# Loading and converting the f64 weights of a fused attention, FFN and MoE kernel in pairs of pieces

## The chip, the cores and the metric

The kernel runs on one core of a Trainium2 chip. The metric is the device time of one execution in microseconds (us). Engine names: PE is TensorE, DVE is VectorE, ACT is ScalarE, POOL is GpSimd, SP is SyncE, which issues nearly all DMAs here.

## The reference

Three stages follow one another. `moe_w_in` and `moe_w_out` arrive as f64, all else as f32.

```python
# attention: q, k, v are (4, 8, 576, 64); a mask lets block i of 64 rows see blocks 0..i
scores = scale * np.matmul(q, k.transpose(0, 1, 3, 2))
attn = exp(scores - max) / (sum + 1e-09);  x = attn @ v        # -> 2304 tokens x 512
# dense FFN: w_in (512, 2048), w_out (2048, 512), both f64
h = x @ w_in;  g = where(h > 0, h, exp(min(h, 0)) - 1);  x = g @ w_out
# MoE: tokens with x @ w_skip > 0 go to the best of 8 experts, the others pass through
out[do_compute] = xc + gate_w * (relu(xc @ w1[e]) @ w2[e])
```

## The kernel before

**Stages.** Tokens go through the FFN in nine chunks of 256 (`c` = 0 to 8). Attention is cut into units of one batch, head pair and block pair, which run between the matmuls of the FFN chunks. The experts follow, in a tail of their own. Chunk 0 and chunk 1 use the f32 weights directly (`twi`, `two` as lhs or rhs of f32 matmuls, PE groups `h<-xt,twi` and `y<-two,g`). From chunk 2 on, the weights are split into f16 high and low parts (`win`, `wout`), and a matmul becomes three f16 ones.

**The raw weights.** An f64 is two int32 words. Each of the 16 weight blocks `j` (eight of `w_in`, eight of `w_out`) is loaded raw in two pieces of 512 KB, so there are 32 pieces `x`. `raw_load` (L460) issues one on SP into a place of 128 x 1024 int32: three places that serve any piece (two buffers of the tag `pay`, one of `wt`), and eight (`wo0` to `wo7`) that are later the targets of the `w_out` blocks and may serve pieces before that. A piece of `w_in` has all 512 rows and 128 columns, so its contiguous runs are 1 KB; one of `w_out` has 128 whole rows, runs of 4 KB. `conv` (L486) makes 512 f32 columns of a piece with three DVE instructions, one `TENSOR_SCALAR` and two `SCALAR_TENSOR_TENSOR`. Each of the last two reads what the one before it wrote. Within a block, the first half of the columns is ready when its own piece is converted.

**What sets the order.** The program is not run in the order in which it is written. Every operation is recorded with an estimated duration (`Recorder`, L35), and `Recorder.order` (L152) lists them anew per engine from the dependences, the estimates and a due time that follows the place in the program. Each engine then runs its own list strictly in order, and waits at the head of it block all behind. `conv_step` (L1291) records a conversion and the loads around it: it runs at most five pieces ahead. A load of piece `x` that is recorded after the conversion of piece `x-4` waits for that conversion (end of `raw_load`).

**Around it.** SP's list mixes the raw weight pieces with `raw<-in_q/k/v` (f32 rows of 64, runs of 256 bytes), the DMA transposes `kt`, `qt`, `et` and `x2t`, the copies `qt<-qt`, and `vflat`, a whole batch of `v` that ACT squares and sums (`vmax`, L621) so that `vscale(1)` (L631) can take a maximum on DVE (`col<-col`). `l2` (L923) multiplies block `f` of `g` by block `f` of `w_out` for both halves of the tokens. `post` (L943) writes the chunk's rows through a `pay` buffer. `ahead_gather` (L1080) uses one `pay` buffer between the posts of chunk 7 and of chunk 8.

```python
def conv_step():                       # L1291
    x = nload[0]
    load_to(x + 1)
    conv(x)
    load_to(min(nraw[0] + 2, x + 5))
    nload[0] += 1
```

Of the kernel before, what the change touches and what calls it, by code (L numbers as in the profile page):

```python
# [347 lines left out]
def tile_kernel(ctx, tc, q, k, v, w_in, w_out, w_skip, w_gate, w1, w2, out):  # L348
# [109 lines left out]
    CONV = {}  # L458

    def raw_load(x):  # L460

        if not RING:
            RING.append(True)
            RFREE.extend((99, pool.tile([128, 1024], I32, tag=tag, bufs=bufs, name="rw")) for pool, tag, bufs in ((mo, "pay", 2), (mo, "pay", 2), (wp, "wt", 1)))
            RFREE.extend((16 + 2 * i, wp.tile([128, 1024], I32, tag=f"wo{i}", bufs=1, name="rw")) for i in range(8))
        ok = [r for r in RFREE if r[0] > x]
        if not ok:
            return False
        place = min(ok, key=lambda r: r[0])
# [16 lines left out]
    def conv(x):  # L486

        j, m = divmod(x % 16, 2)
        kind = "wi" if x < 16 else "wo"
        if m == 0:  # L490
            TW[kind, j] = wp.tile([128, 1024], I32, tag=f"{kind}{j}", bufs=1, name=f"t{kind}{j}")
        t = TW[kind, j]
        place = RAWW.pop(x)
        RFREE.append(place)
        raw = place[1].rearrange("p (f two) -> p f two", two=2)
        lo, hi = raw[:, :, 0], raw[:, :, 1]
        if kind == "wi":
            dst = t.rearrange("p (k f) -> p k f", k=4)[:, :, m * 128:(m + 1) * 128]
            lo, hi = (a.rearrange("p (k f) -> p k f", k=4) for a in (lo, hi))
        else:  # L500
            dst = t[:, m * 512:(m + 1) * 512]
        rc.vector.tensor_scalar(out=dst, in0=hi, scalar1=0x07FFFFFF, scalar2=3, op0=ALU.bitwise_and, op1=ALU.logical_shift_left)
        rc.vector.scalar_tensor_tensor(out=dst, in0=hi, scalar=-(1 << 30), in1=dst, op0=ALU.bitwise_and, op1=ALU.bitwise_or)
        rc.vector.scalar_tensor_tensor(out=dst, in0=lo, scalar=29, in1=dst, op0=ALU.logical_shift_right, op1=ALU.bitwise_or)
        CONV[x] = len(rc.steps) - 1

# [35 lines left out]
    def split_win(j):  # L542
        t = wp.tile([128, 2, 1024], F16, tag="wt" if j == 0 else f"wi{j - 1}", bufs=1, name=f"win{j}")
# [32 lines left out]
    def split_wout(j):  # L576
        t = wp.tile([128, 2, 1024], F16, tag="wi7" if j == 0 else f"wo{j - 1}", bufs=1, name=f"wout{j}")
# [209 lines left out]
    def h_unit(b, p, i):  # L787
# [14 lines left out]
        elif HL.get(("wo", 7)) is not None and nu[0] % 3 == 0:  # L802
            pool, tag, bufs = wp, "wo7", 1
        else:
            pool, tag, bufs = ap, "ehl", 2
        HP[b, p, x] = pool.tile([128, n, nk, 2, 128], F16, tag=tag, bufs=bufs, name="ehl")
# [537 lines left out]
    for x in range(8):  # L1344
# [607 lines left out]
```

## Time and profile before

| | |
|---|---|
| runs shown | 752.17, 742.56, 750.12 us; median 750.12 us |
| the profiled execution | 746.02 us, of which the span of the trace is 743.9 us |
| mean granted TensorE clock | 0.968 of full speed |
| PE busy | 679.4 us (91% of the span) |
| DVE, ACT busy | 578.7 us (78%), 513.9 us (69%) |
| DMA | 134.52 MB, mean 181 GB/s |

The span falls into three stretches. Up to some 140 us the weights are loaded and chunk 0 runs. From there to some 580 us PE is busy nearly without a break. The experts' tail fills the rest. A busy engine is not yet the one that sets the time: for that, the rows below say what each wait ended with.

### The profile page before, as it was taken

The numbers are of one execution on the slowest core, as the hardware profiler recorded it, in microseconds if no ns is written. First come the engines' busy times: TensorE is split into PE (matmuls) and PEld (weight loads), VectorE is DVE, ScalarE is ACT, GpSimd is POOL, SyncE is SP. The second block draws the span as 40 slices with busy tenths as digits, with TensorE's granted clock in tenths as the row PEclk, the third lists the DMA queues.
The fourth block names the chain that finished last, engine by engine and source line by source line (L and its number), as shares of the span: only waits on it lengthen the run. The fifth ranks groups of instructions, "written<-read, shape, count | busy, mean of one in ns | idle before, by whom it ended". The sixth has DMA issues, their size and how long they took to land.

```text
span 743.9 us, 17734 instructions
## 1 busy us (share of the span) xinstructions
PE 679.4 (91%) x6665; PEld 466.1 (63%) x6665; DVE 578.7 (78%) x1664; ACT 513.9 (69%) x1090; POOL 83.4 (11%) x122
## 2 busy tenths in 40 slices
PE   4689997999999899999999999989999989997894
PEld 3467543775476657657657658657575768675673
DVE  5987989897899797989869966999687634554752
ACT  5876656999797785788758846775365727685782
POOL 2000000010000100000100010100113124143211
PEclk9669999899999999999999999999999999999998
DMA  9999999967787989699656559726267486799941
GB/s 271 270 262 294 292 280 207 203 119 149 145 170 147 172 177 198 122 172 195 112 90 135 90 96 281 277 78 207 57 199 211 124 180 138 200 244 252 272 127 16
DMA packets 267355, 134.52 MB, mean 181 GB/s; under 512 B 234539, under 2 KB 243765, under 8 KB 266736
## 3 DMA queue, kind: packets, MB, share of 16 engines
q1 hardware_dynamic: 263056, 125.69, 72.7%
q0 software_dynamic: 4192, 7.49, 4.7%
q8 instruction: 57, 0.93, 0.5%
q14 instruction: 50, 0.41, 0.2%
HBM read 74.38 MB, written 12.75 MB: 117 GB/s over the span
## 4 chain that ended last, share of the span: by engine, by line
PE 45%; DMA 19%; issue 16%; DVE 12%; ACT 3%; POOL 2%; SPq 1%; POOLq 0%; another core or an unknown queue 0%; DVEq 0%; ACTq 0%
PE h L310 18%; PE y L310 17%; DMA et<-ehl 6%; DMA gp<-pay_d,lists 5%; PE s L310 4%; PE xps L310 3%; DVE ehl L310 2%; DMA rw<-in_moe_w_out_dram 2%; DMA out_dram<-o,gp 2%; DVE two L310 1%; DVE mx L310 1%; DMA vflat<-in_v_dram 1%; POOL out_dram L1684 1%; DMA lst_d<-li,si 1%; DVE el L310 1%
## 5 line engine op out<-in xcount | busy, mean ns | idle before, releaser
L310 PE MATMUL h<-xt,win 128*128 128x256 f16 x1344 | 158.7, 273 | 2.2 <-DVE el L310 2.1
L310 PE MATMUL y<-wout,g 128*128 128x512 f16 x672 | 155.1, 379 | 0.0
L310 PEld LDWEIGHTS <-win 128*128 128x128 f16 x1344 | 128.6, 98 | 23.9 <-issue 2.7
L310 PEld LDWEIGHTS <-g 128*128 128x128 f16 x672 | 63.4, 98 | 68.0 <-issue 1.4
L310 ACT ACTIVATE e<-s,mx 128x512 f32<-128x512 f32 (+4 forms) x160 | 82.2, 516 | 21.4 <-DVE ehl L310 11.5
L310 ACT ACTIVATE ehl<-e,su 128x512 f16<-128x512 f32 (+4 forms) x160 | 79.8, 549 | 13.0 <-DVE su L310 7.5
L310 DVE SCALAR_TENSOR_TENSOR ehl<-e,su,ehl 128x512 f16<-128x512 f32 (+4 forms) x160 | 81.1, 538 | 2.7 <-ACT ehl L310 2.7
L310 DVE TENSOR_REDUCE mx<-s 128x1 f32<-128x512 f32 (+4 forms) x160 | 74.3, 475 | 10.0 <-PE s L310 9.3
L310 PE MATMUL s<-kt,qt 128*128 128x384 f16 (+5 forms) x384 | 68.9, 310 | 9.6 <-ACT e L310 7.9
L310 PE MATMUL xps<-et,vt 128*64 128x128 f16 (+1 forms) x1440 | 51.5, 220 | 14.2 <-DMA et<-ehl 8.2
L310 PEld LDWEIGHTS <-vt 128*64 128x64 f16 x1440 | 41.1, 115 | 35.5 <-issue 22.9
L310 PE MATMUL h<-xt,twi 128*128 128x256 f32 x256 | 62.1, 396 | 0.8 <-DVE g L310 0.8
L310 PE MATMUL y<-two,g 128*128 128x512 f32 x128 | 61.0, 615 | 1.9 <-DVE two L310 1.9
L310 ACT ACTIVATE g<-el,col 128x512 f16<-128x512 f32 x56 | 40.1, 717 | 29.6 <-DVE el L310 29.3
L310 PEld LDWEIGHTS <-p 128*128 128x128 f16 x984 | 47.8, 99 | 14.5 <-issue 6.1
L310 PEld LDWEIGHTS h<-xt,twi 128*128 128x128 f32 x256 | 49.2, 198 | 8.0 <-DVE g L310 1.2
L310 ACT ACTIVATE el<-h,col 128x512 f32<-128x512 f32 x56 | 38.2, 683 | 15.5 <-PE h L310 13.9
L310 DVE SCALAR_TENSOR_TENSOR g<-el,col,g 128x512 f16<-128x512 f32 x56 | 41.6, 744 | 3.5 <-ACT g L310 3.3
L1511 DVE SCALAR_TENSOR_TENSOR p<-p,n,p 128x1024 f16<-128x1024 f32 x32 | 40.7, 1280 | 4.4 <-ACT p L1510 4.2
L310 PEld LDWEIGHTS <-qt 128*128 128x128 f16 (+1 forms) x384 | 27.6, 104 | 26.2 <-issue 12.4
L310 DVE SCALAR_TENSOR_TENSOR el<-h,col,el 128x512 f32<-128x512 f32 x56 | 41.8, 746 | 1.2
L310 DVE TENSOR_TENSOR hh<-r,hh 128x256 f16<-128x256 f32 x36 | 14.8, 422 | 35.0 <-ACT hh L310 35.0
(233 smaller groups left out, 1143.6 us busy)
## 6 DMA issues: line engine op xcount, KB each, us to landing
p<-in_moe_w_dram SPq DMA_DIRECT2D x49, 512.0 KB, 6.1
rw<-in_moe_w_in_dram SPq DMA_DIRECT2D x16, 512.0 KB, 6.2
rw<-in_moe_w_out_dram SPq DMA_DIRECT2D x16, 512.0 KB, 6.3
pb<-in_moe_w_dram SPq DMA_DIRECT2D x10, 512.0 KB, 4.5
vflat<-in_v_dram SPq DMA_DIRECT2D x4, 1152.0 KB, 6.7
out_dram<-pay SPq DMA_DIRECT2D x18, 256.0 KB, 2.8
pay_d<-pay SPq DMA_DIRECT2D x18, 256.0 KB, 2.7
raw<-in_k_dram SPq DMA_DIRECT2D x16, 256.0 KB, 3.6
```

What stands on the lines that cost most here:

```text
L310: rec.call(e, time, lambda: getattr(self.real, op)(*args, **kw), reads, writes, dma)
L1511: rc.call("dve", 1.2, lambda: nc.vector.scalar_tensor_tensor(out=half(1), in0=raw.t, scalar=sc, in1=half(0), op0=ALU.mult, op1=ALU.subtrac ...
L1684: i = nc.gpsimd.indirect_dma_start(out=out.rearrange("n (h d) -> (n h) d", h=m), out_offset=bass.IndirectOffsetOnAxis(ap=ts, axis=0), in_= ...
```

## The change

A load is now counted as a half `u` of a pair `x` (`x, m = divmod(u, 2)`), and a pair is one weight block. The places become pairs: `pay`, `wt` and `wo` are each one large tile, cut into parts, so there are six places of two pieces (12 pieces) where there were 11 single ones. `wt` grows by one part; among the experts' buffers one of 23 is given up for it. A piece of `w_in` has 256 rows and 256 columns, so its runs are 2 KB. The first four pairs are still converted half by half, 512 columns at a time. From the fifth on (`WHOLE = 4`) one conversion covers 1024 columns and needs both pieces. `conv_step` may run six pieces ahead (`AHEADW`). The uses of the old tags further down take parts of the large tiles; `ahead_gather` takes part 0 of `pay`, and `post` part `t`.

```diff
-    def raw_load(x):
+    def raw_load(u):
+        x, m = divmod(u, 2)
...
-            RFREE.extend((16 + 2 * i, wp.tile([128, 1024], I32, tag=f"wo{i}", bufs=1, name="rw")) for i in range(8))
+            RFREE.extend((99, BIGT[t].rearrange("p a x -> p (a x)")) for t in ("pay", "wt"))
+            RFREE.extend((8 + 2 * i, BIGT["wo"][:, 2 * i:2 * i + 2].rearrange("p a x -> p (a x)")) for i in range(4))
+        if m == 0:
+            ok = [r for r in RFREE if r[0] > x]
...
-            src = w_in32[:, 2 * f0:2 * (f0 + 128)].rearrange("(k p) x -> p k x", p=128)
+            src = w_in32[256 * m:256 * m + 256, 512 * j:512 * j + 512].rearrange("(k p) x -> p k x", p=128)
...
-        if x - 4 in CONV:
-            rc.steps[-1][4].add(CONV[x - 4])
+        if u - 4 in CONV:
+            rc.steps[-1][4].add(CONV[u - 4])
...
+        whole = x >= WHOLE
         if m == 0:
...
+        elif whole:
+            return
...
+        if not whole:
+            t = t[:, 512 * m:512 * m + 512]
+            raw = raw[:, 512 * m:512 * m + 512]
...
+        if whole:
+            CONV[u + 1] = CONV[u]
+        if whole or m:
+            RFREE.append(RAWW.pop(x))
...
-        load_to(x + 1)
+        load_to((x | 1) + 1 if x // 2 >= WHOLE else x + 1)
         conv(x)
-        load_to(min(nraw[0] + 2, x + 5))
+        load_to(min(nraw[0] + 2, x + AHEADW))
...
-        pay = mo.tile([128, 1024], F32, tag="pay", bufs=2, name="pay")
+        pay = BIGT["pay"][:, t].bitcast(F32)
```

SP's list, at the place where the first key transpose of the attention follows the first loads, stood like this before (`rw` is a raw piece, `wg` the router's gate, `vflat` the second batch of `v` for `vmax`, `raw` rows of `k`, `q` or `v`):

```order
L310 DMA rw<-in_moe_w_in_dram 128x4x256 x2
L310 DMA raw<-in_k_dram 128x8x64
L310 DMA wg_79<-in_moe_w_gate_dram 128x4x8
L310 DMA vflat<-in_v_dram 128x2304
L310 DMA raw<-in_q_dram 128x8x64
L310 DMA raw<-in_v_dram 128x8x64
L310 DMA rw<-in_moe_w_in_dram 128x4x256
L310 DMA_TRANSPOSE kt<-k_194 128x8x128
```

It stands like this now (`wo` and `pay` as targets are raw pieces in parts of these tiles):

```order
L310 DMA wo<-in_moe_w_in_dram 128x2x512 x2
L310 DMA raw<-in_q_dram 128x8x64
L310 DMA raw<-in_v_dram 128x8x64
L310 DMA wo<-in_moe_w_in_dram 128x2x512
L310 DMA_TRANSPOSE kt<-k_186 128x8x128
L310 DMA wo<-in_moe_w_in_dram 128x2x512
L310 DMA raw<-in_k_dram 64x8x64
L310 DMA wo<-in_moe_w_in_dram 128x2x512
L310 DMA wg_79<-in_moe_w_gate_dram 128x4x8
L310 DMA wo<-in_moe_w_out_dram 128x1024
L310 DMA pay<-in_moe_w_out_dram 128x1024
L310 DMA_TRANSPOSE qt<-qq 128x8x128
```

Two more pieces of `w_in` took the place of `vflat`, which moved behind, and two first halves of `w_out` pairs moved ahead of a query transpose.

DVE's list, where chunk 0's `g` (the activation's result) meets the conversions, stood like this before (`col<-col` is the maximum of `vscale(1)`, which reads what ACT makes of the last `vflat`):

```order
L310 SCALAR_TENSOR_TENSOR g<-g,h 128x512
L310 TENSOR_REDUCE col<-col 128x1
L310 TENSOR_SCALAR twi_310<-rw 128x4x128
L310 SCALAR_TENSOR_TENSOR twi_310<-rw,twi_310 128x4x128
L310 SCALAR_TENSOR_TENSOR g<-g,h 128x512
L310 SCALAR_TENSOR_TENSOR twi_310<-rw,twi_310 128x4x128
```

In the changed kernel the same `col<-col` stands behind the first two `w_out` pairs (`wo<-wo` is a conversion out of a raw part of `wo` into another, `mx` a row maximum of the attention):

```order
L310 TENSOR_SCALAR wo<-wo 128x1024
L310 SCALAR_TENSOR_TENSOR wo<-wo 128x1024
L310 TENSOR_SCALAR su<-su 128x2
L310 TENSOR_SCALAR wo<-wo 128x1024
L310 SCALAR_TENSOR_TENSOR wo<-wo 128x1024
L310 SCALAR_TENSOR_TENSOR g<-g,h 128x512
L310 SCALAR_TENSOR_TENSOR wo<-wo 128x1024
L310 SCALAR_TENSOR_TENSOR g<-g,h 128x512
L310 SCALAR_TENSOR_TENSOR wo<-wo 128x1024
```

The reduction moved from between the last two `w_in` blocks to behind two whole `w_out` pairs and all eight `g` of chunk 0.

## Rows read from the trace of the kernel before

**Rows 1.** Stages: PE, PEld, DVE, ACT, POOL busy (instructions), PEclk, DMA share, GB/s

```profile
60.00:80.00 20.00, 19.22 (x105) 16.11 (x105) 15.26 (x30) 11.87 (x22) 0.00 (x0) 1.00 1.11 327
80.00:100.00 20.00, 18.14 (x76) 8.26 (x74) 19.38 (x40) 10.74 (x22) 0.00 (x0) 0.91 1.11 262
100.00:120.00 20.00, 17.37 (x109) 7.85 (x108) 18.54 (x42) 11.48 (x26) 0.00 (x0) 1.00 1.07 258
140.00:160.00 20.00, 20.00 (x247) 16.24 (x246) 17.31 (x56) 19.36 (x51) 1.36 (x3) 1.00 0.92 156
```

**Rows 2.** Chain that ended last, 71 to 121 us: start, us, what

```profile
71.16 7.47 DMA rw<-in_moe_w_out_dram
...
91.95 4.52 PE y L310 x6
...
104.81 4.42 DMA rw<-in_moe_w_out_dram
...
116.01 5.07 DMA et<-ehl
```

**Rows 3.** DVE groups by shape, 0 to 125 us: busy us, mean ns | idle before

```profile
L310 DVE SCALAR_TENSOR_TENSOR two<-rw,two 128x512 int32<-128x512 int32 x32 | 21.5, 685 | 0.0
L310 DVE TENSOR_SCALAR two<-rw 128x512 int32<-128x512 int32 x16 | 6.7, 423 | 2.3 <-DMA rw<-in_moe_w_out_dram 2.3
```

**Rows 4.** DVE timeline: start, us, what [idle before <-releaser]

```profile
61.39 1.42 DVE L310 SCALAR_TENSOR_TENSOR twi<-rw,twi 128x512 int32<-128x512 int32 x2
66.57 0.16 DVE L310 TENSOR_REDUCE col<-col 128x1 f32<-128x4 f32 x1 [3.17 <-ACT vflat L310]
71.74 0.42 DVE L310 TENSOR_SCALAR two<-rw 128x512 int32<-128x512 int32 x1
82.26 2.49 DVE L310 SCALAR_TENSOR_TENSOR two<-rw,two 128x512 int32<-128x512 int32 x4
118.60 0.42 DVE L310 TENSOR_SCALAR two<-rw 128x512 int32<-128x512 int32 x1
120.59 0.68 DVE L310 SCALAR_TENSOR_TENSOR two<-rw,two 128x512 int32<-128x512 int32 x1
```

**Rows 5.** The page's part 5: two f32 sizes of one DVE operation, busy, mean ns

```profile
L310 DVE SCALAR_TENSOR_TENSOR g<-el,col,g 128x512 f16<-128x512 f32 x56 | 41.6, 744 | 3.5 <-ACT g L310 3.3
L1511 DVE SCALAR_TENSOR_TENSOR p<-p,n,p 128x1024 f16<-128x1024 f32 x32 | 40.7, 1280 | 4.4 <-ACT p L1510 4.2
```

**Rows 6.** Stages with `w_in` pieces (first) or `w_out` pieces in flight; columns as Rows 1

```profile
66.00:68.00 2.00, 1.89 (x9) 1.33 (x7) 1.26 (x4) 1.72 (x5) 0.00 (x0) 1.00 1.10 348
75.00:79.00 4.00, 4.00 (x21) 3.51 (x20) 3.11 (x8) 2.73 (x7) 0.00 (x0) 1.00 1.06 387
```

**Rows 7.** SP's own timeline: start, us, what it issued

```profile
71.16 4.72 SPq L310 DMA_DIRECT2D rw<-in_moe_w_out_dram  x4
113.94 0.52 SPq L310 DMA_DIRECT2D rw<-in_moe_w_out_dram  x1
```

**Rows 8.** All raw pieces, issue to landing in us

```profile
DMA to landing us min/median/max: 4.4/6.3/8.0
```

**Rows 9.** PE timeline, chunk 0's second product and chunk 1's start

```profile
80.41 3.60 PE L310 MATMUL y<-two,g 128*128 128x512 f32 x8
91.95 4.52 PE L310 MATMUL y<-two,g 128*128 128x512 f32 x6 [1.03 <-DVE two L310]
115.00 1.12 PE L310 MATMUL y<-two,g 128*128 128x512 f32 x2 [0.84 <-DVE two L310]
122.34 3.70 PE L310 MATMUL y<-two,g 128*128 128x512 f32 x8
134.22 3.00 PE L310 MATMUL h<-xt,twi 128*128 128x256 f32 x8
```

**Rows 10.** SP's timeline near the end of chunk 8: the early gather, then the first post

```profile
566.72 3.92 SPq L310 DMA_TRANSPOSE mxt<-gpa  x2
577.70 0.34 SPq L310 DMA_DIRECT2D out_dram<-pay  x1
```

More of the change, by code (lines that the diff above doesn't have):

```diff
@@ L481, in raw_load, with conv @@
         rc.sync.dma_start(out=dst, in_=src)
-        if x - 4 in CONV:
-            rc.steps[-1][4].add(CONV[x - 4])
-        return True
-    def conv(x):
-        j, m = divmod(x % 16, 2)
-        kind = "wi" if x < 16 else "wo"
+        if u - 4 in CONV:
+            rc.steps[-1][4].add(CONV[u - 4])
+        return True
+    def conv(u):
+        x, m = divmod(u, 2)
+        kind = "wi" if x < 8 else "wo"
+        j = x % 8
+        whole = x >= WHOLE
         if m == 0:
-            TW[kind, j] = wp.tile([128, 1024], I32, tag=f"{kind}{j}", bufs=1, name=f"t{kind}{j}")
+            TW[kind, j] = wp.tile([128, 1024], I32, tag=f"wi{j}", bufs=1, name=f"twi{j}") if kind == "wi" else wo(j, I32)
+        elif whole:
+            return
@@ L492, in conv @@
         t = TW[kind, j]
-        place = RAWW.pop(x)
-        RFREE.append(place)
+        place = RAWW[x]
         raw = place[1].rearrange("p (f two) -> p f two", two=2)
+        if not whole:
+            t = t[:, 512 * m:512 * m + 512]
+            raw = raw[:, 512 * m:512 * m + 512]
         lo, hi = raw[:, :, 0], raw[:, :, 1]
[L497 to L505, printed above, removed]
+        rc.vector.tensor_scalar(out=t, in0=hi, scalar1=0x07FFFFFF, scalar2=3, op0=ALU.bitwise_and, op1=ALU.logical_shift_left)
@@ L802, in h_unit @@
         elif HL.get(("wo", 7)) is not None and nu[0] % 3 == 0:
[L803 removed]
+            pool = None
         else:
             pool, tag, bufs = ap, "ehl", 2
[L806 removed]
+        if pool:
+            HP[b, p, x] = pool.tile([128, n, nk, 2, 128], F16, tag=tag, bufs=bufs, name="ehl")
+        else:
+            HP[b, p, x] = wo(7, F16)[:, 0:256 * n * nk].rearrange("p (n k a c) -> p n k a c", n=n, k=nk, a=2)
         if n == 1:
@@ L1343, in tile_kernel @@
         on_a(4 + 2 * x, conv_step)
-    for x in range(8):
-        on_q(0, x, lambda x=x: conv_to(2 * (x + 4)))
-    for x in range(8, 12):
-        on_q(0, x, lambda x=x: conv_to(24 + 2 * (x - 7)))
+    for x in range(12):
+        on_q(0, x, lambda x=x: conv_to(2 * (x + 4 + (x > 7))))
     for b in range(1, 4):
@@ L1435, in __init__ @@
             self.t = t
-    FREE = [Place(f"p{x}") for x in range(23)]
-    m2p = list(FREE)
+    m2p = [Place(f"p{x}") for x in range(22)]
+    FREE = m2p + [Place(None, BIGT["wt"][:, 1].bitcast(F32))]
     junk = Place("jk")
@@ L1538, in tile_kernel @@
     prep(EARLY[2], 1)
-    FREE += [Place(None, wp.tile([128, 1024], F32, tag=t, bufs=1, name=f"pb{x}")) for x, t in enumerate(["wt"] + [f"wi{i}" for i in range(7)])]
+    FREE.append(Place(None, wt()))
+    FREE += [Place(None, wp.tile([128, 1024], F32, tag=f"wi{i}", bufs=1, name=f"pb{i}")) for i in range(7)]
     load_half(5, 0)
     load_half(5, 1)
-    FREE += [Place(None, wp.tile([128, 1024], F32, tag=t, bufs=1, name=f"pd{x}")) for x, t in enumerate(("wi7", "wo0", "wo1"))]
+    FREE.append(Place(None, wp.tile([128, 1024], F32, tag="wi7", bufs=1, name="pd0")))
+    FREE += [Place(None, wo(x)) for x in range(2)]
     rc.urgent = True
@@ L1898, in tile_kernel @@
     rc.urgent = False
-    FREE += [Place(None, mo.tile([128, 1024], F32, tag="pay", bufs=2, name=f"pc{x}")) for x in (1, 2)]
+    FREE += [Place(None, BIGT["pay"][:, x].bitcast(F32)) for x in range(2)]
     for h in "s5-0 s5-1 l1-0".split():
```

51 lines of the change are left out of this document (30 added, 21 removed).

## The prediction

> **What bounds the kernel now.** I read the stages first, because a share over the whole span says little here. From 140 us on PE is busy 20.0 of 20 us [rows 1], so what is gained before that point reaches the end almost whole, and what the change does after it can hardly show. Up to there no engine is full: PE is busy 17.4 to 19.2 us of 20, DVE up to 19.4, and the DMA engines' share is above 1 throughout. The chain of waits says who ends a wait: in chunk 0's second product it goes from the landing of a `w_out` piece (7.47 us, later 4.42) over DVE's conversions to the matmuls `y`, and near the end over a transpose of the attention (5.07 us) [rows 2]. PE itself waits for a converted block twice, 1.03 and 0.84 us [rows 9]. DVE waits 2.3 us in all for pieces of `w_out` [rows 3], and once 3.17 us for ACT's sum over the last batch of `v`, with a conversion and two `g` queued behind [rows 4]. So loads and conversions share the bound, and the question is which of the two the change moves.
>
> **DVE's instructions.** The first four blocks keep six instructions each, the other twelve go from six to three: 36 fewer. Four of them in a row take 2.49 us, one alone 0.685 [rows 3, 4], so one starts (2.49 - 0.685) / 3 = 0.602 us after another. From 512 to 1024 columns an operation of this kind grows by 1280 - 744 = 536 ns [rows 5], so 0.602 - 0.536 = 0.066 us is paid per instruction, and 36 x 0.066 = 2.4 us goes. Two that depend on each other take 1.42 us [rows 4], 0.735 apart, or 0.2 us per instruction: 7.2 us is the upper bound. I take the low price, since the order mostly puts other work between dependent ones. Only the eight `w_out` blocks lie in the stretch where DVE is full: 24 x 0.066 = 1.6 us on the path. A conversion of 1024 columns should take 0.42 + 0.27 = 0.69 and 0.685 + 0.536 = 1.22 us.
>
> **The loads.** Sixteen pieces of `w_in`, 16 x 0.524 = 8.39 MB, get runs of 2 KB for 1 KB. While only such pieces are in flight the rate is 348 GB/s, and with `w_out` pieces (4 KB runs) 387 [rows 6]. That is 24.1 us for 8.39 MB, or 21.7 at the other end; halfway, 368 GB/s, 22.8. I take 1.3 us, between 0 and 2.4. It is not hidden, since the queue is full: SP issues four pieces in 4.72 us [rows 7] and each lands 4.4 to 8.0 us later [rows 8].
>
> The Trainium skill ("DMA: Bandwidth & Descriptors", Specifications) gives 512 B as the smallest transfer at line rate, so 1 KB and 2 KB should be alike. By it this term is 0 instead of 1.3 us; the rates just named differ by 11% above that size and speak against it, though other transfers share those windows.
>
> **The place of the second halves.** I counted the bytes of SP's list ahead of a load, in either order. The first `w_out` block is complete with 20.73 MB now, 21.01 before: 0.28 MB less, 1.0 us at 0.28 MB per us. The last block's second piece ends at 32.55 MB now, 32.29 before: 0.9 us later. Against the 1.3 us above, the first comes 2.3 us sooner and the last 0.4 sooner.
>
> **The first product's end.** DVE no longer stands at `col<-col` for 3.17 us. But it then reaches the first `w_out` pair earlier than its second half lands. Before, that piece was issued at 71.16 and landed 7.47 us later, at 78.65 [rows 2, 7]; now about 76.3. DVE did its first such conversion at 71.74 [rows 4]; without the stall it stands there near 70. So the 3.17 us turn into a wait of some 6 us for a DMA, at a new place, with two `g` and the row maxima queued behind it. Converted after another 0.60 + 1.13 + 1.13 us and one `g` of 0.6, block 0 is ready at about 79.8; `y` began at 80.41 [rows 9]. Gain here: 0.6 us. The reduction `col<-col` itself comes after both pairs, near 85 us. The last `vflat` stands after 21.8 MB in SP's list; pieces at that place were issued at 71 to 76 us [rows 7], so it is summed by then, about 83. Its wait then costs nothing; the cover is thin, 2 us.
>
> **Whole pairs.** A half can no longer be converted while the other lands. Before, the last half was converted from 118.60 to 120.59 + 0.68 = 121.27 [rows 4], with other work in between, 2.7 us. Now it is 0.60 + 1.13 + 1.13 plus one 0.53 between them, 3.4 us after the landing: 0.7 us worse, and at blocks where PE waits the two matmuls on the first half wait too. The last piece was issued at 113.94 [rows 7]; now 113.5. With the median landing of 6.3 us its conversion ends at 113.5 + 6.3 + 3.4 = 123.2; the last block's `y` began at 122.34 [rows 9], then held by the attention's transpose. That is 0.9 us later; with 4.4 us landing it is 1.0 sooner, with 8.0 it is 2.6 later.
>
> **The rest.** `post(8,0)` and the early gather now share a buffer. The gather's transposes are issued from 566.72 to 570.6 and land in at most 5.4 us, 576; the post's first DMA follows at 577.70 [rows 10], so the wait just fits, at a cost of 0; without that cover, a few tenths. The attention's operations are ordered differently up to about 370 us. PE had no idle time at 140 to 160, and little later, that they could give back; I take 0, plus or minus 3 us.
>
> **The sum.** If loads bound chunk 0: -1.3 (rate) + 0.9 (place) + 0.7 (whole pairs) = +0.3 us. If DVE does: -1.6 - 3.2 = -4.8 us. DVE waits for pieces in both, and the new wait is one for a DMA, so I stay near the first: -1.0 us. The profiled execution's own 746.02 becomes 745.0. It lies between the runs, whose median is 750.12; the mean of the three and the profile is 747.7, and I take that as the level: 746.7 us.
>
> **The rivals.**
> 1. *DVE was the bound* (-4.8, 742.9 us). For it: 19.4 of 20 us busy at 80 to 100 [rows 1] and the conversions in the chain. Against: its waits there end with a DMA.
> 2. *The second halves come too late* (+4, 751.7 us). An odd half waits for the conversion two pairs back, where an even one may run ahead. Pairs follow one another by (118.60 - 71.74) / 7.5 = 6.2 us [rows 4]; two intervals less a conversion of 3.4 leave 9.0 us for issue and landing. A landing of 6.3 fits with SP's own time; from about 7.5 on it doesn't, and at 8.0 [rows 8] each of four pairs is 1.0 us late. For it: landings reach 8.0. Against: the median.
> 3. *Longer runs bring nothing* (+0.3 us for -1.0, so 748.0 us). The mechanism is that rates differ by what else is in flight, not by the run: then the term of 1.3 us is 0. For it: both windows of rows 6 hold other traffic. Against: 348 and 387 are steady. The page named above would have it so.
>
> That the change does not do what it says is out: the order shows 1024-column instructions.
>
> **How the numbers follow.** Forecast 0.45, rival 1 0.25, rival 2 0.2, rival 3 0.1. The range goes from rival 1 to rival 2, 742.9 to 751.7, and by 3 us on either side for a median of runs that spread by 10: 740 to 754.5. The forecast alone is 744 to 749. Two per cent, 15 us, is about what a measurement can tell from no change; it needs twice any term here, plus the granted clock falling or rising for a long stretch: faster 0.04, same 0.93, slower 0.03.
>
> **What would show it.** Right: DVE has 36 instructions fewer, of 0.69 and 1.22 us; no wait for `vflat` near 65 us; a wait of 4 to 7 us for a piece before the first `w_out` pair; DVE's waits for pieces grow from 2.3 us to over 5; chunk 1's first `h` (134.22 before [rows 9]) at 132 to 135. Wrong: that `h` at 130 or earlier, or DVE's waits for pieces as small as before (then DVE was the bound); or waits of a microsecond and more at four or five later pairs (rival 2); a rate of the `w_in` pieces of 348 GB/s or less (rival 3); or a difference made after 140 us.

## The result

The changed kernel takes 750.73 us (median of 20 runs, 746.1 to 761.4) against 745.40 for the kernel before on the same chip. The ratio is 1.0086, 95% interval 1.0062 to 1.0110. So it is slower by some 6.4 us (5.3 between the medians) where 1.0 us faster was forecast. The time lies inside the predicted range, and within 2% of before, but the sign is wrong. The profiled execution of the changed kernel, 759.81 us, is one of the two slow ones of its 20, so its trace lies further from that of before than the medians do, and a second trace of the same kernel (`e1_after_again`, 758.04 us) is read beside it.

The stages of the changed kernel's trace (windows, columns as in [rows 1]), and under them both stretches up to 575 us:

```profile
60.00:80.00 20.00, 17.51 (x82) 14.98 (x83) 14.79 (x21) 13.52 (x26) 0.00 (x0) 1.00 1.09 311
80.00:100.00 20.00, 17.84 (x97) 8.92 (x97) 18.79 (x31) 13.63 (x26) 0.00 (x0) 1.00 0.94 249
100.00:120.00 20.00, 14.02 (x101) 6.68 (x99) 15.62 (x26) 10.78 (x24) 0.00 (x0) 1.00 1.11 248
120.00:140.00 20.00, 17.00 (x144) 9.40 (x145) 18.18 (x74) 14.78 (x35) 0.61 (x3) 0.85 0.95 203
...
0.00:140.00 140.00, 105.20 (x712) 69.25 (x713) 114.08 (x273) 93.50 (x200) 4.75 (x42) 0.89 1.04 260
140.00:575.00 435.00, 423.01 (x3950) 283.51 (x3950) 369.05 (x1110) 314.44 (x695) 30.26 (x42) 1.00 0.72 155
```

The same two stretches of the kernel before:

```profile
0.00:140.00 140.00, 109.75 (x716) 72.34 (x717) 119.41 (x321) 96.66 (x209) 4.56 (x41) 0.87 1.08 265
140.00:575.00 435.00, 425.06 (x3978) 282.80 (x3977) 370.00 (x1102) 314.24 (x690) 32.26 (x45) 1.00 0.71 156
```

Before 140 us PE was idle for 140 - 109.75 = 30.2 us, and is now for 34.8; from there to 575 us 9.9 became 12.0. That is 6.6 us more idle time (some 4.7 in the second trace), half of it between 100 and 120 us, where PE is busy 14.0 of 20 us for 17.4 [rows 1]. The experts' tail begins with the first `ahp` matmul. On PE's timeline it stood at 579.37 us before and stands at 585.72 now, 6.3 us later:

```profile
585.72 2.17 PE L1153 MATMUL ahp<-mxt,p 128*128 128x128 f16 x36
```

The conversions of `w_out` in the changed kernel (DVE's groups: instruction and count, busy us, mean ns, idle time ahead of it and what ended it), to stand against [rows 3]:

```profile
L310 DVE SCALAR_TENSOR_TENSOR wo<-wo 128x1024 int32<-128x1024 int32 x8 | 9.7, 1216 | 0.0
L310 DVE TENSOR_SCALAR wo<-wo 128x1024 int32<-128x1024 int32 x4 | 2.8, 694 | 0.9 <-DMA wo<-in_moe_w_out_dram 0.8
L310 DVE TENSOR_SCALAR wo<-wt 128x1024 int32<-128x1024 int32 x2 | 1.4, 694 | 2.4 <-DMA wt<-in_moe_w_out_dram 2.4
L310 DVE TENSOR_SCALAR wo<-pay 128x1024 int32<-128x1024 int32 x2 | 1.4, 690 | 1.2 <-DMA pay<-in_moe_w_out_dram 1.2
```

The sizes were right: 0.69 and 1.22 us. The waits for pieces add up to 0.8 + 2.4 + 1.2 = 4.4 us, where they were 2.3. DVE's timeline shows where DVE now stands:

```profile
70.07 0.69 DVE L310 SCALAR_TENSOR_TENSOR g<-g,h 128x512 f32<-128x512 f32 x1 [1.43 <-ACT g L310]
74.44 0.69 DVE L310 SCALAR_TENSOR_TENSOR k<-raw,k 128x512 f16<-128x512 f32 x1 [3.68 <-ACT k L310]
...
76.84 0.68 DVE L310 TENSOR_SCALAR wo<-wo 128x1024 int32<-128x1024 int32 x1
...
86.57 0.15 DVE L310 TENSOR_REDUCE col<-col 128x1 f32<-128x4 f32 x1
...
100.77 0.69 DVE L310 TENSOR_SCALAR wo<-wo 128x1024 int32<-128x1024 int32 x1 [0.83 <-DMA wo<-in_moe_w_out_dram]
108.26 0.69 DVE L310 TENSOR_SCALAR wo<-wt 128x1024 int32<-128x1024 int32 x1 [2.20 <-DMA wt<-in_moe_w_out_dram]
115.84 0.69 DVE L310 TENSOR_SCALAR wo<-pay 128x1024 int32<-128x1024 int32 x1 [1.20 <-DMA pay<-in_moe_w_out_dram]
121.73 0.69 DVE L310 TENSOR_SCALAR wo<-wt 128x1024 int32<-128x1024 int32 x1 [0.21 <-DMA wt<-in_moe_w_out_dram]
...
124.12 1.23 DVE L310 SCALAR_TENSOR_TENSOR wo<-wt,wo 128x1024 int32<-128x1024 int32 x1
```

The stall of 3.17 us at `col<-col` [rows 4] is gone, and a stall of 3.68 us at `k<-raw,k` stands in its place, 1.43 us at a `g` before it (4.37 and 1.43 in the second trace). ACT's timeline says why:

```profile
70.54 2.12 ACT L310 ACTIVATE vflat<-vflat 128x2304 f32<-128x2304 f32 x1 [0.50 <-DMA vflat<-in_v_dram]
...
72.66 0.58 ACT L310 ACTIVATE g<-h 128x512 f32<-128x512 f32 x1
73.78 0.63 ACT L310 ACTIVATE k<-raw 128x512 f16<-128x512 f32 x1 [0.54 <-DMA raw<-in_k_dram]
```

The `vflat` that the change moved back is squared by ACT at 70.54 us, in the middle of chunk 0's `g`, and the scaling of `k` queues behind it and behind its own late piece. PE's timeline in chunk 0's second product (to compare with [rows 9]):

```profile
81.27 3.60 PE L310 MATMUL y<-wo,g 128*128 128x512 f32 x8
...
92.11 3.70 PE L310 MATMUL y<-wo,g 128*128 128x512 f32 x8 [1.45 <-DVE wo L310]
...
120.18 5.37 PE L310 MATMUL y<-wo,g 128*128 128x512 f32 x8 [1.81 <-DVE wo L310]
127.20 3.70 PE L310 MATMUL y<-wo,g 128*128 128x512 f32 x8
...
137.84 2.50 PE L310 MATMUL h<-xt,twi 128*128 128x256 f32 x5
```

The first `y` is 0.9 us later than before, the last block's 4.9, and chunk 1's first `h` 3.6 (134.22 before).

### The profile page after: what moved, and what is told of

Same layout as the page of the kernel before. It is cut to its first block, busy times and chain, and to the rows that moved or that the text cites. A ratio compares the mean times of both kernels' runs of the same rounds, so it can differ in the third digit from the quotient of the medians.

```text
span 757.7 us, 17701 instructions
## 1 busy us (share of the span) xinstructions
PE 683.5 (90%) x6665; PEld 469.1 (62%) x6665; DVE 576.6 (76%) x1628; ACT 513.5 (68%) x1090; POOL 80.4 (11%) x122
## 4 chain that ended last, share of the span: by engine, by line
PE 31%; issue 16%; DMA 13%; DVE 7%; POOL 3%; ACT 1%; POOLq 0%; SPq 0%; another core or an unknown queue 0%; DVEq 0%; ACTq 0%
PE h L310 13%; PE y L310 12%; DMA wo<-pay_d,lists 5%; DMA et<-ehl 3%; PE s L310 2%; PE xps L310 2%; DMA out_dram<-wo 2%; POOL out_dram L1704 1%; POOL wo L310 1%; DVE el L310 1%; DVE ehl L310 1%; DVE n L1498 1%; PE ahp L1153 1%; DMA et<-wo 1%; DMA qt<-qq 1%
## 5 line engine op out<-in xcount | busy, mean ns | idle before, releaser
L310 PE MATMUL y<-wo,g 128*128 128x512 f16 (+1 forms) x716 | 196.6, 422 | 3.3 <-DVE wo L310 3.3
L310 PE MATMUL h<-xt,win 128*128 128x256 f16 x1176 | 140.9, 275 | 2.0 <-DVE rts L310 2.0
L310 PEld LDWEIGHTS <-win 128*128 128x128 f16 x1176 | 113.4, 98 | 21.0 <-issue 2.4
L310 ACT ACTIVATE ehl<-e,su 128x512 f16<-128x512 f32 (+4 forms) x130 | 65.0, 549 | 11.7 <-DVE su L310 3.4
L310 DVE SCALAR_TENSOR_TENSOR ehl<-e,su,ehl 128x512 f16<-128x512 f32 (+4 forms) x130 | 65.9, 536 | 3.3 <-ACT ehl L310 3.3
L310 PEld LDWEIGHTS <-p 128*128 128x128 f16 x888 | 43.7, 100 | 13.1 <-issue 5.3
L310 PEld LDWEIGHTS <-hh 128*64 128x64 f16 (+1 forms) x432 | 30.8, 115 | 21.8 <-ACT hh L310 3.4
L310 DVE TENSOR_TENSOR hh<-r,hh 128x256 f16<-128x256 f32 x36 | 14.8, 422 | 37.2 <-ACT hh L310 37.2
L310 PEld LDWEIGHTS y<-wo,g 128*128 128x128 f32 x128 | 24.0, 195 | 27.6 <-issue 23.4
```

Of the source, the lines that this page charges most:

```text
L310: rec.call(e, time, lambda: getattr(self.real, op)(*args, **kw), reads, writes, dma)
```

## The experiments

The edits below are shown shortened. Six theories stand in the expectations. S: the second half of a pair lands late, and whole conversions wait for it (rival 2). D: of that, the odd half's wait for the conversion two pairs back. W: a conversion of 1024 columns can't begin on its first half. L, first called R: the planner's order, as a whole, sets the time. P: places that are freed only as pairs. A: the sixth piece ahead. (In `e3_oldshape` and `e4_longruns` the letter L stands for something else, that the new shape of a `w_in` piece is what costs.) The table has for each kernel its ratio to the kernel before on the same chip, and from its trace: the end of chunk 0's last `y`, the issue of the last `w_out` piece, the start of chunk 1's first `h`, PE's idle time before 140 us and from there to 575, and the start of the tail (us).

| kernel | ratio, 95% interval | last `y` | last piece | `h` | idle | tail from |
|---|---|---|---|---|---|---|
| before | 1 | 126.0 | 113.9 | 134.2 | 30.2 + 9.9 | 579.4 |
| e4_longruns | 1.0007 (0.9979–1.0034) | 128.3 | 116.5 | 136.2 | 34.7 + 10.3 | 582.8 |
| e11_jit_before | 1.0010 (0.9971–1.0049) | 132.4 | 117.0 | 138.3 | 34.0 + 10.0 | 582.9 |
| e14_jit_before2 | 0.9985 (0.9955–1.0014) | 130.5 | 118.7 | 137.0 | 33.9 + 10.8 | 582.0 |
| changed | 1.0086 (1.0062–1.0110) | 130.9 | 116.2 | 137.8 | 34.8 + 12.0 | 585.7 |
| e1_after_again | 1.0087 (1.0058–1.0117) | 129.5 | 114.8 | 136.9 | 33.6 + 11.2 | 583.0 |
| e3_oldshape | 1.0130 (1.0067–1.0193) | 133.0 | 119.9 | 141.4 | 36.7 + 14.1 | 592.1 |
| e7_sixops | 1.0085 (1.0052–1.0119) | 127.8 | 115.0 | 136.8 | 34.0 + 11.3 | 581.3 |
| e17_threethree | 1.0071 (1.0042–1.0100) | 132.6 | 117.0 | 140.1 | 35.5 + 11.5 | 585.7 |
| e13_pool_after | 1.0133 (1.0089–1.0177) | 136.1 | 119.4 | 143.3 | 37.0 + 14.8 | 591.1 |
| e12_jit_after | 1.0047 (1.0015–1.0079) | 128.3 | 115.9 | 136.2 | 33.3 + 11.2 | 583.9 |
| e15_jit_after2 | 1.0069 (1.0034–1.0103) | 132.1 | 116.5 | 138.0 | 33.4 + 12.2 | 587.1 |
| e9_nodep | 1.0057 (1.0026–1.0088) | 116.4 | 102.3 | 132.9 | 29.9 + 13.3 | 581.6 |
| e10_wo_whole | 1.0014 (0.9983–1.0046) | 127.8 | 112.3 | 133.4 | 32.4 + 12.2 | 580.8 |
| e2_halves | 1.0050 (1.0013–1.0087) | 117.5 | 97.6 | 132.2 | 32.0 + 13.0 | 580.7 |
| e5_halves5 | 1.0127 (1.0077–1.0177) | 123.8 | 110.1 | 130.0 | 30.7 + 15.2 | 585.8 |
| e6_ahead5 | 1.0131 (1.0088–1.0173) | 137.1 | 120.0 | 140.0 | 35.3 + 12.8 | 586.9 |
| e8_wi_whole | 0.9949 (0.9916–0.9981) | 116.5 | 97.4 | 130.7 | 29.0 + 7.6 | 572.7 |
| e16_jit_wi | 1.0015 (0.9980–1.0050) | 115.6 | 100.4 | 133.1 | 31.3 + 10.8 | 579.1 |
| e18_jit_wi2 | 0.9913 (0.9879–0.9948) | 114.3 | 98.9 | 132.9 | 30.7 + 9.1 | 576.8 |

Before the single runs, one reading of the whole table. `e4_longruns` has exactly the order of before and the same median, yet its trace has 4.8 us more idle time on PE, and its tail begins 3.4 us later. The shape of the `w_in` pieces differs between those two, so not all of that need be chance; the two traces of the changed kernel differ in nothing, and are 2.0 us apart in idle time and 2.7 in the tail's start. So one trace is good for some 2 to 5 us, and the 6.6 us between the first two traces above can't be taken at its face. Over all rows the ratio goes with the sum of PE's idle time (correlation 0.84), and less with the end of the last `y` (0.59). It is the idle time after 140 us that carries this: that part alone gives 0.84, the part before 140 us 0.59.

### The change once more, and its parts at an unchanged order

> The changed kernel once more, for a trace whose clock is that of the kernel before. Measured so far: 1.0086 of before. Theory S (the second half of a pair lands late and whole conversions wait for it): about 1.009, chunk 1's first h some 3.5 us later than the 134.22 of before, DVE's waits for w_out pieces 4 to 6 us in all, PE's waits for converted blocks (y<-DVE wo) over 3 us. Theory R (the planner's new order of the attention costs the time): the same ratio, but PE's extra idle time lies mostly after 140 us, in waits for transposes, and chunk 1's first h within 1.5 us of before.

It came out the same again, 1.0087. Both theories had this ratio; `h` at 136.9 is nearer to S.

```diff
-            src = w_in32[:, 2 * f0:2 * (f0 + 128)].rearrange("(k p) x -> p k x", p=128)   # before
+            src = w_in32[256 * m:256 * m + 256, 512 * j:512 * j + 512]...                 # e4_longruns
```

> The kernel before with only the shape of a w_in piece changed (256 rows, 256 columns, runs of 2 KB), single places and conversions of 512 columns as before. PE, ACT and SP keep exactly the order of before. If longer runs are worth 1.3 us: 0.998. If they bring nothing: 1.000. If the new shape itself costs (theory L): 1.006 to 1.010. w_in pieces alone in flight should move at 360 to 390 GB/s against 348 if the run length matters.

No gain is seen: 1.0007. The interval reaches down to 0.9979, so it does not exclude the 1.3 us (0.998) either. In the windows of [rows 6] the rate was 340 GB/s at 66 to 68 us for 348 before, and 320 at 75 to 79 for 387:

```profile
66.00:68.00 2.00, 2.00 (x11) 1.75 (x10) 0.00 (x0) 1.80 (x1) 0.00 (x0) 1.00 1.12 340
75.00:79.00 4.00, 4.00 (x22) 3.14 (x21) 4.00 (x8) 2.10 (x6) 0.00 (x0) 1.00 1.18 320
```

The second window holds `w_out` pieces, whose shape is the same in both kernels. So what is in flight at a given moment differs from one execution to the next by more than the 348 and 387 of the prediction differ. The Trainium skill ("DMA: Bandwidth & Descriptors", Specifications) has 512 B as the smallest transfer at line rate, by which 1 KB and 2 KB are alike. This run does not speak against that, and its interval is too wide to show it.

The same edit undone in the changed kernel (the `-` line above put into it, with the target cut to match):

> The changed kernel with only the shape of a w_in piece put back (all rows, 128 columns, runs of 1 KB). PE, ACT and SP keep exactly the changed kernel's order. If longer runs are worth the 1.3 us of the prediction: 1.010 to 1.011. If they bring nothing: 1.0086. If the new shape itself is what costs (theory L): 0.999 to 1.003.

1.0130, with a wide interval that overlaps that of the changed kernel. The longer runs may be worth a little there (its first `y` is at 84.6 us); that the new shape is what costs is out in both orders.

```diff
-        rc.vector.tensor_scalar(out=t, in0=hi, ...)          # 1024 columns, one step
+        for h in range(2):                                   # same step, two instructions
+            nc.vector.tensor_scalar(out=t[:, 512 * h:512 * h + 512], in0=hi[:, 512 * h:...], ...)
```

> The changed kernel, its order on every engine kept exactly, with each conversion of 1024 columns issued as six instructions of 512 (each of its three steps for both halves): 36 instructions more. If the price of an instruction counts (0.066 us by the prediction, 24 on the path): 1.0087 + 0.002 = 1.011. If DVE's time in the conversions is not on the path: 1.0087 again. If the single instruction over both halves is what costs, because it can't begin on the first: 1.003 to 1.006.

1.0085, the same as with three. The interval, 0.3% or 2.5 us on either side, is wider than the price of 1.6 us that was put on them, so that price is neither seen nor excluded.

```diff
 # step 1, 2, 3 of a whole conversion: (instruction, half)
-((0, both),), ((1, both),), ((2, both),)
+((0, 0), (1, 0), (2, 0)), ((0, 1), (1, 1)), ((2, 1),)
```

> The changed kernel, its order on PE, ACT and SP kept exactly; in each whole conversion the first step makes all three instructions of 512 columns of the first half, the second and third step those of the second half. The first half no longer waits for the second piece, and y's matmuls on it can begin up to 2 us sooner. Theory W (that a conversion can't begin on the first half is the harm): y's waits for wo fall from 3.5 us to about 1, ratio 1.003 to 1.006. Theory L (the order as a whole): 1.007 to 1.010, since other waits take the place.

`y`'s waits fell as W said; the ratio, 1.0071, did not follow clearly (its interval takes in W's upper end and no gain). PE's waits up to 140 us, in this kernel (its conversions stand at L522):

```profile
PE s L310 <- ACT e L310: 6.6, 6, 1.8
PE xps L310 <- DMA et<-ehl: 4.8, 3, 3.1
...
PE y L310 <- DVE wo L522: 1.4, 2, 1.1
```

and in the changed kernel (the trace of e1_after_again):

```profile
PE s L310 <- ACT e L310: 5.7, 6, 1.8
PE y L310 <- DVE wo L310: 3.5, 3, 1.8
PE xps L310 <- DMA et<-ehl: 2.9, 4, 0.9
```

The 2.1 us that `y` gained stand again at the attention's transposes (+1.9) and its exponentials (+0.9), as far as two single traces can tell. In this order W's wait is real, and no gain from taking most of it away is shown.

```diff
-        rc.sync.dma_start(out=dst, in_=src)
+        nc.gpsimd.dma_start(out=dst, in_=src)    # w_out pieces; recorded as a step of SP still
```

> The changed kernel with the sixteen w_out pieces issued by POOL in place of SP; the order of all else on SP, PE, DVE and ACT is exactly the changed kernel's. On POOL, which is nearly idle then, a piece waits for its place alone and not behind transposes of the attention. Theory D (late second halves are the harm): y's waits for wo fall from 3.5 us to below 1, DVE's waits for w_out pieces from 4.6 to below 1.5, and the ratio to 1.002 to 1.005. Theory L (the order of the attention is the harm): y's waits go, the ratio stays at 1.007 to 1.010, and other waits take their place. If earlier pieces delay the transposes: above 1.010, with PE's waits for et longer than 9 us.

DVE never waits for a `w_out` piece any more, `y` still waits 2.9 us for DVE, and the kernel is no faster, 1.0133. Waits up to 140 us, first of DVE, then of PE:

```profile
DVE qq L310 <- ACT qq L310: 8.8, 4, 5.5
DVE g L310 <- ACT g L310: 5.7, 3, 2.8
```

```profile
PE h L310 <- DVE g L310: 8.3, 2, 7.2
...
PE y L310 <- DVE wo L310: 2.9, 3, 1.4
```

Five pieces go out together at 53 to 56 us. The rows of `q`, issued by SP at 52.7, land 12 us later, ACT waits for them with `g` queued behind, and `h` stands for 7.2 us at once. ACT's timeline:

```profile
64.73 0.63 ACT L310 ACTIVATE qq<-raw 128x512 f16<-128x512 f32 x1 [5.33 <-DMA raw<-in_q_dram]
```

The third case of the expectation, but with `q` in the place of the transposes; that the five pieces are what delayed the rows is read off the times and not tested. So nothing that was tried at the changed kernel's own order gives the time back.

### Parts that make the planner order anew

```diff
-        if whole:
-            CONV[u + 1] = CONV[u]
```

> The changed kernel without its two lines that set CONV of the odd half, so that the second piece of a pair no longer waits for the whole conversion two pairs back (its place in SP's list is then set by the free place alone). All conversions from the fifth pair on still of 1024 columns. In SP's list the last w_out piece stands after 30.6 MB and three et transposes (changed kernel 32.5 and five). Theory D (that wait is the harm, rival 2 of the prediction): 0.996 to 1.003, DVE's waits for w_out pieces below 2 us, last y of chunk 0 at 121 us or before. Theory W (a conversion that can't begin on the first half is the harm by itself): 1.006 to 1.010.

Without that wait in the plan the loads come sooner, as D has it: the last `w_out` piece is issued 12 to 14 us sooner, at 102.3, no `y` waits, and the last one ends at 116.4 us. The price is not: 1.0057, whose interval takes in a gain of 0.6% on the change and none. What was gained by `h` (132.9 for 136.9 and 137.8) is in part lost after 140 us, where PE waits 6.9 + 3.5 us for transposes (4.2 + 1.2 and 5.7 + 0.6 in the two traces of the changed kernel, 6.4 in the kernel before):

```profile
PE xps L310 <- DMA et<-ehl: 6.9, 8, 1.3
PE xps L310 <- DMA et<-wo: 3.5, 3, 2.2
```

The planner brings `y` forward and the attention moves back, and later matmuls then wait for it.

```diff
-    WHOLE, AHEADW = 4, 6
+    WHOLE, AHEADW = 16, 6            # e2_halves; e5_halves5: 16, 5; e6_ahead5: 4, 5
```

> WHOLE = 16: every block is converted half by half, 512 columns at a time, with the pairs of pieces, the longer runs of w_in and six pieces ahead all kept. The planner orders it anew. Theory S: the first half is converted while the second lands, so most of the loss goes: 0.998 to 1.003 of before, chunk 1's first h at 133 to 136 us, DVE's waits for w_out pieces below 3 us. Theory R: no reason for a gain, any value between 0.995 and 1.012, with the loss after 140 us. Theory P (pairs as places, freed only together, hold the loads back): stays at 1.006 to 1.010, and SP's issues of the last w_out pieces stay as late as in the changed kernel, 115 us.

> WHOLE = 16 and AHEADW = 5: pairs as places and the longer runs are kept, but every conversion is of 512 columns and only five pieces run ahead, as before. SP's list has the raw pieces nearly where the kernel before has them (the first w_out piece after 19.4 MB in both, the last after 31.5 against 32.3 MB). If the pairs as such cost nothing: 0.998 to 1.002. If freeing a place only as a pair costs (theory P): 1.004 to 1.008.

> The changed kernel with AHEADW = 5 in place of 6: whole conversions as in the change, five pieces ahead as before. With it the last w_out piece stands later in SP's list, after 33.5 MB and seven et transposes (changed kernel: 32.5 MB and five; before: 32.3 and five). Theory S (whole conversions wait for second halves, and the loads behind them wait in turn): 1.010 to 1.018, worse than the change, chunk 0's last y later than 129 us. Theory A (the sixth piece ahead is the harm, since two w_out pieces are loaded at 31 us ahead of what chunk 0's attention needs): 0.999 to 1.004.

`e2_halves` behaves like `e9_nodep`: `y` is done at 117.5, PE idles 13.0 us after 140, and the ratio is 1.0050, above what S said. `e5_halves5`, whose loads stand nearly as before, has the earliest `h` of all (130.0) and the most idle time after 140 us (15.2): 1.0127, above all that was expected of it. With `e6_ahead5` it speaks against A, and leaves the pairs as places (P) or L; but in `e2_halves` P's sign, loads held back to 115 us, is absent (97.6). `e6_ahead5` came out as S had it, 1.0131, with the last `y` at 137.1.

```diff
-        whole = x >= WHOLE
+        whole = x in range(4, 8)     # e8_wi_whole, w_in alone; e10_wo_whole: range(8, 16)
```

> Whole conversions for the blocks of w_in alone (fifth to eighth pair), halves for all of w_out, six ahead. In SP's list the w_out pieces come earlier than in the change: the last after 29.3 MB and three et transposes, against 32.5 and five. Theory S (the whole conversions of w_out): near the 1.005 of the kernel with halves everywhere, chunk 0's last y below 122 us, DVE's waits for w_out pieces below 1.5 us. If the w_in blocks' whole conversions are the harm: 1.008 to 1.011.

> The reverse of the kernel with whole conversions for w_in alone: halves for all of w_in, whole conversions for w_out, with the odd half's wait; last w_out piece after 31.5 MB and five et transposes. Theories D and W both: 1.006 to 1.012, waits for w_out pieces of 3 us and more. Theory L (the planner's order scatters by a per cent whatever the edit): anywhere from 0.995 to 1.013.

`e8_wi_whole` is faster than both kernels, 0.9949. Up to its first `y`, at 80.4 us, it runs as the changed kernel does, but then no `y` waits, the last is done at 116.5, and nothing is given back after 140 us:

```profile
80.42 3.60 PE L310 MATMUL y<-wo,g 128*128 128x512 f32 x8
...
114.53 1.98 PE L310 MATMUL y<-wo,g 128*128 128x512 f32 x4
130.69 1.97 PE L310 MATMUL h<-xt,twi 128*128 128x256 f32 x8
```

```profile
0.00:140.00 140.00, 110.97 (x794) 74.80 (x795) 120.96 (x319) 97.95 (x216) 4.95 (x43) 0.89 1.06 267
140.00:575.00 435.00, 427.43 (x3957) 283.26 (x3956) 370.26 (x1102) 313.64 (x687) 32.42 (x46) 1.00 0.72 158
```

That is 29.0 and 7.6 us of idle time, the least of all. `e10_wo_whole` is at 1.0014, though its `w_out` is converted whole and its last `y` is late: against D and W, which had 1.006 and more. The four kernels with or without whole conversions in either half (1.0050, 0.9949, 1.0014, 1.0086) don't add up as two separate effects would. Either the two act on each other, or it is as L says: each edit draws a new order, and the order scatters.

### The same versions in other orders

To get at an edit's own price, each version was given further orders by a shift of one number of the planner, in nothing else:

```diff
-            return 0.48, b / 360e3 * (2 if run < 512 else 1)
+            return 0.48, b / 350e3 * (2 if run < 512 else 1)   # e11, e12, e16; e14, e15, e18: 370e3
```

> The kernel before with nothing changed but the planner's idea of the DMA rate, 350 in place of 360 bytes per ns, which reorders the attention and the loads. It measures how far an order alone moves the time. Theory L: 1.005 to 1.015 or below 0.996. If a small shift of the plan is harmless: 0.998 to 1.003.

> The changed kernel with the same shift of the planner's DMA rate; the last w_out piece after 32.3 MB and six et transposes. Theory D: 1.006 to 1.012 as without the shift, waits for w_out pieces of 4 us and more. Theory L: a value off by more than 0.4% from 1.0087 on either side, down to 0.997.

> The kernel before with the planner's DMA rate at 370 bytes per ns: a third order of the same program (first 1.000, second 1.001). Theory L: the orders scatter by about half a per cent, as the changed versions do, so 0.995 to 1.008. If the kernel before is robust: 0.998 to 1.003.

> The changed kernel with the planner's rate at 370: a third order of it (first 1.0087, second 1.0047). If the edit itself costs: 1.004 to 1.010. Theory L: anything from 0.996 to 1.012.

> The kernel with whole conversions for w_in alone (0.9949 in its first order), with the planner's rate at 350: a second order. If halves for w_out are worth the gain by themselves: 0.992 to 0.998. Theory L: 0.998 to 1.008, so that the first was a lucky order.

> The kernel with whole conversions for w_in alone, planner's DMA rate at 370: its third order (0.9949, 1.0015 so far). If halves for w_out are as good as the kernel before on average: 0.995 to 1.002, so that the mean of three lies 0.5 to 1% below that of the change. If the two versions differ by their orders alone: 1.003 to 1.010.

| version | three orders | mean |
|---|---|---|
| before | 1, 1.0010, 0.9985 | 0.9998 |
| changed | 1.0086, 1.0047, 1.0069 | 1.0067 |
| whole conversions for `w_in` alone | 0.9949, 1.0015, 0.9913 | 0.9959 |

The kernel before kept to what was expected of a robust one; `e12_jit_after` fell just below the 1.006 of D; the third version was at 1.0015 once, as L had it, and at 0.9913, better than anything expected. No order of the changed kernel is as fast as the slowest of before, or as the slowest of the third version. The intervals of single orders do overlap (1.0015 to 1.0079 for `e12_jit_after`, 0.9971 to 1.0049 for `e11_jit_before`), but the means of three differ by 0.7%, with plus or minus 0.4% as the spread of the orders gives it. So the edit has a price of its own, 0.7% or 5 us over orders, on top of which an order lies up to 0.1 to 0.6% off its version's mean. Theory L in its strong form, that the edit only drew a bad order, is out. And the comparison with the third version, which keeps the pairs, the longer runs and the sixth piece ahead, points to the whole conversions of `w_out`: without them the kernel is 1.1% faster on average, with plus or minus 1.1% on the same reckoning, so this is less sure. In all three orders of the third version the last piece is issued at 97 to 100 us, for 115 to 117 in the changed kernel's, and chunk 0's last `y` ends at 114 to 117, for 128 to 132. DVE's waits for `w_out` pieces between 60 and 125 us go the same way: in the three orders of each, 4.4, 5.4 and 8.7 us in the changed kernel, 2.3, 3.5 and 5.0 before, 0.2, 0 and 0.4 in the third version. But single orders speak against making this the whole price: `e10_wo_whole` has 3.9 us of these waits and is at 1.0014, and `e2_halves`, which converts nothing whole, and `e9_nodep` have none and are at 1.0050 and 1.0057.

**What stays open.** How the price comes about within an order. At the changed kernel's order no single wait that was taken away gave it back. Over the changed kernel's orders (six traces, `e7` and `e17` among them) PE has 45.7 us of idle time up to 575 and the tail begins at 584.5; over before's (four) it is 43.5 and 581.8. That is 2.2 to 2.7 us of the 5. PE's order in the tail is the same in both but for one of before's orders; from its start to the end of the profiled execution it took 162.6 to 175.0 us (means 166.8 before, 169.4 after), a difference within that scatter, so the rest can't be placed. That scatter goes with the granted clock: over the 20 traces the tail's length falls as its mean clock rises (correlation -0.81). At 0.98 of full speed it took 162.4 to 164.8 us (three traces), at 0.94 or 0.95 172.6 to 175.0 (four, both of the changed kernel's first order among them), and 162.6 to 169.4 at the 0.97 of the four of before. The clock is not what the edit costs: over all runs of the changed kernel's three orders (`e1_after_again`, `e12_jit_after`, `e15_jit_after2`) its mean is 0.973, and 0.972 for the kernel before beside them. Nor were `e5_halves5` and `e2_halves` given further orders, so what the pairs cost without any whole conversion isn't known.

## Why the prediction was wrong

**What bounds the kernel.** Right in that the ratio goes with PE's idle time before the experts. Wrong in that what the change does after 140 us can hardly show: PE's idle time there was 9.9 us before, 11.2 to 12.2 in the changed kernel's traces and 7.6 to 15.2 over all kernels, and the ratio goes with it more closely than with the part before 140 us. And too narrow in taking the bound to be loads and conversions of `w_out`. In `e9_nodep` and `e2_halves` the last `y` ended 9.7 and 8.5 us sooner than in the kernel before, and both were slower than it. The attention's chain of transposes, exponentials and row loads is as close to the bound as `y` is.

**DVE's instructions.** Durations right (0.69 and 1.22 us). The term of 1.6 us on the path was not seen: with all 36 back, `e7_sixops` is at 1.0085 for 1.0086, give or take 2.5 us. Rival 1 (DVE was the bound) is out by the time: DVE had its 36 instructions fewer and no `col<-col` stall, and the kernel was not 4.8 us faster but slower.

**The loads.** The term of 1.3 us was not seen in the order of before (`e4_longruns`, 1.0007), though its interval doesn't exclude it. What fails is the source of the term: rows 6 compared two moments with other traffic, and took the difference for that of the runs. In this rival 3 was right.

**The first product's end.** A step that failed early, and for little. The stall at `col<-col` went, and it did turn into another, but not into one of 6 us for a `w_out` piece: DVE stood 1.43 us for a `g` and 3.68 for ACT's scaling of `k`, because the moved `vflat` then stood in ACT's way at 70.54 us and `k`'s rows were late. The first `w_out` conversion began at 76.84 without a wait, and `y` at 81.27, where 79.8 was forecast. That is 1.5 us. The prediction asked what becomes of DVE, which no longer waits for `vflat`; it didn't ask whom `vflat` meets on ACT at its new place. This wait is that of one order, though. In `e12_jit_after` and `e15_jit_after2`, the changed kernel in two other orders, DVE does not wait for `k` there, and the wait for a piece ahead of the first pair is found, shorter than it was forecast (`e12_jit_after` first):

```profile
76.98 0.69 DVE L310 TENSOR_SCALAR wo<-wo 128x1024 int32<-128x1024 int32 x1 [2.50 <-DMA wo<-in_moe_w_out_dram]
76.70 0.69 DVE L310 TENSOR_SCALAR wo<-wo 128x1024 int32<-128x1024 int32 x1 [3.94 <-DMA wo<-in_moe_w_out_dram]
```

**The place of the second halves, and whole pairs.** This is the step that failed: +0.9 and +0.7 us, sized by bytes ahead of a piece in SP's list. The last conversion was to end at 123.2; it ended at 124.12 + 1.23 = 125.35, and the last `y` began at 127.20, 4.0 us after it should. Over three orders each, the edit costs 5 us, where these two terms make 1.6 even with no gain set against them, and the version that keeps the pairs but converts `w_out` by halves is some 8 us faster on average, give or take as much, where whole pairs were to cost 0.7. Bytes were the wrong measure, since SP's list is a chain of waits. SP issued the last pieces here, the second of them at 116.2, not at the 113.5 of the prediction:

```profile
115.29 1.32 SPq L310 DMA_DIRECT2D wt<-in_moe_w_out_dram  x2
```

SP's longest waits between 60 and 125 us (in total, times, longest) are for the attention's exponentials and row maxima, behind whose transposes the pieces stand:

```profile
SPq L310 <- ACT ehl L310: 6.4, 1, 6.4
SPq L310 <- DVE mx L310: 6.3, 3, 4.2
SPq L310 <- DVE ehl L310: 5.0, 2, 4.4
```

In the kernel before the longest was for conversions of `w_out`:

```profile
SPq L310 <- DVE two L310: 8.1, 2, 5.1
```

That wait is absent here, 0.2 us in the second trace and 2.8 and 2.3 in the other two orders; in the third version, where PE waits at most 0.8 us for a conversion of `w_out`, it is 11.6 to 19.1. So in the changed kernel a late piece is hardly held by a conversion while it runs: the planner has put it behind the attention. (In `e7_sixops` and `e17_threethree`, of the same order with the conversions cut up, that wait is 3.5 and 9.0 us, so it is no measure of the loss by itself.) How the pairs and whole conversions make the planner do so, and how much of the 5 us that is, stays open.

Rival 2 came near in time, 751.7 us for 750.73 measured, but partly by luck. It added 4 us to a level of 747.7, where 5.3 over 745.40 was measured, and by its own threshold of 7.5 us a landing of 8.0 makes a pair 0.5 us late and not 1.0. Its condition was not met: the pieces of `w_out` landed within 4.1 to 7.3 us, 4.7 in the median. Of its signs, waits of a microsecond and more were there at two pairs (1.45 and 1.81 us on PE, 2.20 and 1.20 on DVE), not at four or five. `e9_nodep` took its dependence away, which let the planner issue the last piece at 102.3, and left two thirds of the loss; `e17_threethree` took most of `y`'s wait away at no gain that can be seen.

**The rest: the attention's new order, 0 plus or minus 3 us.** Of the 7.4 us between the forecast of -1.0 and the 6.4 measured, 1.4 belong to this order (1.0086 for a mean of 1.0067) and 6.0 to the edit, so the order alone does not explain the miss. But three orders of one version span 0.25 to 1.0%, that is 2 to 8 us, more than the terms for the rate, the place and whole pairs. With such a scatter a forecast of -1.0 us had no more claim than its opposite, and 0.45 on it was too much.

**The signs that were named.** 36 instructions fewer, of 0.69 and 1.22 us: right. No wait for `vflat` near 65 us on DVE: right. A wait of 4 to 7 us for a piece ahead of the first pair: wrong here (2.50 and 3.94 in the other orders). DVE's waits for pieces over 5 us: 4.4. Chunk 1's first `h` at 132 to 135: 137.84, so the loss was there to be seen in it. The buffer that `post(8,0)` shares with the gather: no trace of the changed kernel has a wait there. In `e8_wi_whole` and `e18_jit_wi2`, the two fastest kernels, ACT waits 3.5 us for it, so the cover was as thin as the prediction said.

## What to carry to other kernels

Where a planner makes the order, an edit's price can't be read off one order: shift one harmless number of the planner, take three orders of each version, and compare the means with their spread. Merging two loads' worth of work into one instruction saved nothing that could be measured here, and it ties together both loads, the buffers, and whatever was planned to run on the first half. Where the pieces had arrived (`w_in`, whole conversions in that half alone) it did no harm, 0.996 of before over three orders, with a spread that takes in 1; where DVE waits for the pieces (`w_out`) the runs point to halves, without proving it. Ask of a late load what stands ahead of it in its queue, and what that waits for, before counting bytes. When a stall goes, follow the moved work on every engine that it passes, not only on the one that had stalled.

## What the hardware showed

Two executions with one and the same order on PE (before and `e4_longruns`) differ by 4.8 us in PE's idle time up to 575 us, and two of the changed kernel by 2.0. The tail, nearly the same work in all kernels here, takes 162.4 to 175.0 us. About half of that spread is PE's own busy time in it, which goes with the mean granted clock: 138.8 us at 0.98 of full speed (`e12_jit_after`), 140.3 at 0.97 (before), and 144.6 at 0.95 (changed). A single trace therefore can't carry a difference of half a per cent here. To hand the loads to an idle queue was no gain: with the sixteen pieces on POOL's, DVE's waits for them went from 4.6 us to none, and the kernel came out at 1.0133 for 1.0086, with ACT waiting 5.33 us for row loads of 256 KB that came late.
